# Reordering the head of a gated attention/MLP kernel: warm-up products, the first three transposes and the release of the DMA transposes

## The chip, the cores and the metric

The kernel runs on one core of a Trainium2 chip. The time is the device time of one execution in microseconds (us); the median of several runs is compared. A profiled execution has its own time and, a little shorter, a span from its first to its last instruction; all starts below are us from the beginning of that span. Engines are called PE (TensorE products), DVE (VectorE), ACT (ScalarE), POOL (GpSimd) and SP (SyncE, which here only issues DMAs).

## The reference, cut to what matters

x has 2048 rows (tokens) of 640 bf16 numbers. Two branches are computed from it and mixed by a gate:

```python
def _A_ref(x, wqkv, wo):          # linear attention, 32 heads of 20
    q, k, v = split(x @ wqkv)
    phi = lambda t: jnp.where(t > 0, t + 1, jnp.exp(t)) + 1e-6
    pq, pk = phi(q), phi(k)
    kv = einsum("bhsd,bhse->bhde", pk, v);  z = sum over s of pk
    o = (pq @ kv) / (pq . z + 1e-6)
    return o @ wo

def _B_ref(x, w1, w2, w3, w4):    # mixer with shifted tokens, then an MLP
    h = gelu(layernorm(x) @ w1);  hs = shift tokens of four column groups by 1, -1, 2, -2
    x1 = x + hs @ w2
    return x1 + gelu(layernorm(x1) @ w3) @ w4

g = sigmoid((x * gate_w).sum(-1))
return g * _A_ref(x, ...) + (1 - g) * _B_ref(x, ...)
```

The part that concerns us is the very first stage, the keys: x @ wk, with phi put on it. The gate's sum and a row sum of x are got from the same product, as two extra columns of the weight: `gate_w` and ones.

## The kernel before, in words

The 2048 tokens are 16 chunks of 128. A product on PE contracts over the partition axis, so the key product of a chunk needs x transposed: `xT[:, dc, chunk]`, five blocks of 128 of the 640 features (dc = 0 to 4). The same chunk is also loaded untransposed, as `x_sb`, for later use.

**Two ways to a transposed chunk.** Chunks 0, 1 and 2 are loaded plainly (`load_x`, L155) and turned on PE: `x_tr(c, a, b)` (L322) does five 128x128 transposes, three into PSUM tile `PP[a]` and two into `PP[b]`; DVE copies the three to `xT` and ACT the two (L327, L328). "Turn" below means this. Chunks 3 to 15 are turned by the DMA on the way in: `load_xT` (L158), a DMA transpose issued by SP. They are issued in `late_loads()` (L285) in the order of use, plain loads of `x_sb` between them: chunks 3, 4, x 3, chunks 5, 6, x 4-5, chunk 7, chunks 8-9, x 6-8, chunk 10, chunks 11-12, x 9-11, chunks 13-15, x 12-15, and then the weights wq, w1, wv, wo and w2. POOL's four copies of w1 to `w1x` (L312) stand at its end.

**What holds the DMA transposes.** DVE writes one zero into `xT` at the first element of chunk 3 (L333). The first DMA transpose writes the same place and so waits for that write; the rest stand behind it on SP's queue. DVE works in program order, so the zero is written when DVE has done what stands before it.

**PSUM.** There are four tiles `PP[0]` to `PP[3]`, each 128 x 1024 fp32. `free` lists those not in use; `alloc` takes the first of them, `release` appends one.

**The key product.** `k_mm(c, p, dc)` (L258) is two products, 512 and 130 columns wide (640 features, the gate column and the ones column), accumulated over dc in `PP[p]`. `k_post` (L263) does phi (ACT, then DVE twice) and releases the tile. The gate column of the weight comes from `g5`, a load of gate_w as 5 rows of 128, by one small transpose on PE (L318) and five one-column copies on DVE (L320).

**The order before.** PE first runs six products of zeros (`warm`, L316) while nothing has landed, then the gate's small transpose, the turn of chunk 0, the turn of chunk 1 (which shares `PP[2]` with the first), the key products of chunks 0 and 1 for dc = 0 and 1, the turn of chunk 2, the rest of the key products of chunks 0 to 2, and then chunks 3 to 15 in a loop (L351), with some products of the Gram matrix x^T pk (`g_unit`, L269) between from chunk 5 on. The zero write and `late_loads()` stand after the turn of chunk 0. The program order is kept as written on every engine; the framework adds the semaphore waits. After the keys come the queries (L393, which need wq), the two branches, and the MLP; none of that is touched.

Of the kernel before, what the change touches and what calls it, by code (L numbers as in the profile page):

```python
# [10 lines left out]
BF16 = mybir.dt.bfloat16  # L11
# [5 lines left out]
def kernel(  # L17
# [13 lines left out]
    nc = tc.nc  # L31
    P = 128
    S, D = A_x.shape[1], A_x.shape[2]
# [3 lines left out]
    DC = D // P  # L37
# [18 lines left out]
    def sb(name, cols, dt=BF16):  # L56
        return const.tile([P, cols], dt, name=name)
# [12 lines left out]
    def x1(c):  # L70
        return x1lo[:, c, :] if c < NCH // 2 else x1hi[:, c - NCH // 2, :]
# [5 lines left out]
    wkg = RA[:, 0:DC * KP].rearrange("p (j d) -> p j d", j=DC)  # L77
# [25 lines left out]
    w4z = shs[:, 512:640]  # L103
    w1x = sb("w1x", DC * P)[:].rearrange("p (j d) -> p j d", j=DC)
    kvT = sb("kvT", 6 * GW)[:].rearrange("p (g d) -> p g d", g=6)
    warm = sb("warm", 512)
    ident = sb("ident", P)
    onec = sb("onec", 1)
    mask32 = sb("mask32", 32)
# [2 lines left out]
    g5 = sb("g5", P)  # L112
# [23 lines left out]
    PP = [psum.tile([P, 1024], F32, name=f"pp{i}") for i in range(4)]  # L136
    free = [0, 1, 2, 3]

    def alloc():
        return free.pop(0)  # L140

    def release(i):
        free.append(i)

    mm = nc.tensor.matmul
# [57 lines left out]
    def stats(mv, c, src):  # L203
        st = bst[c % 2]
        h = D // 2

        def a():
            nc.vector.bn_stats(st[:, 0:6], src[:, 0:h])

        def b():  # L210
            nc.vector.bn_stats(st[:, 6:12], src[:, h:D])
            nc.vector.bn_aggr(mv[:, c, :], st[:].rearrange("p (k s) -> p k s", s=6))
        return a, b
# [35 lines left out]
    def phi(dst, src, n, extra=None):  # L249
        e = eb[ecnt[0] % NE]  # L250
        ecnt[0] += 1
        act(e[:, 0:n], src, ACT.Exp)  # L252
        if extra is not None:
            act(extra[0], extra[1], ACT.Copy)
        nc.vector.tensor_scalar(e[:, 0:n], e[:, 0:n], 1.0, 1e-6, op0=ALU.min, op1=ALU.add)  # L255
        nc.vector.scalar_tensor_tensor(dst, src, 0.0, e[:, 0:n], op0=ALU.max, op1=ALU.add)  # L256

    def k_mm(c, p, dc):  # L258
        for (n0, n1) in ((0, 512), (512, KW)):
            mm(PP[p][:, n0:n1], lhsT=xT[:, dc, c * P:(c + 1) * P], rhs=wkg[:, dc, n0:n1],  # L260
               start=(dc == 0), stop=(dc == DC - 1))

    def k_post(c, p):  # L263
        phi(pk[:, c, :], PP[p][:, 0:D], D, (ym[:, c, :], PP[p][:, D:D + 2]))
        release(p)
# [19 lines left out]
    def late_loads():  # L285
        load_xT(3, 4)
        load_xT(4, 5)
        load_x(3, 4)
        load_xT(5, 6)
        load_xT(6, 7)  # L290
        load_x(4, 6)
        load_xT(7, 8)
        load_xT(8, 10)
        load_x(6, 9)
        load_xT(10, 11)
        load_xT(11, 13)
        load_x(9, 12)
        load_xT(13, 16)
        load_x(12, 16)
        rows = lambda w, a, b: w[:, a:b].rearrange("(j p) d -> p j d", p=P)  # L300
        sp.dma_start(wq, rows(A_wqkv, 0, D))
        sp.dma_start(w1, rows(B_w1, 0, D))
        sp.dma_start(wv, rows(A_wqkv, 2 * D, 3 * D))
        sp.dma_start(wo6[0:GW, 0:5, :], A_wo[0:5 * GW, :].rearrange("(g r) d -> r g d", r=GW))
        sp.dma_start(wo6[0:GW, 5, :], A_wo[G5:D, :])
        sp.dma_start(w2[:, 0:4, :], B_w2.rearrange("(g c) d -> c g d", c=CG)[0:P])
        for g in range(4):
            sp.dma_start(w2[32 * g:32 * (g + 1), 4, :], B_w2[CG * g + P:CG * (g + 1), :])
        w1g = w1.rearrange("p k (g c) -> p k g c", c=CG)
        w1x4 = w1x.rearrange("p k (g c) -> p k g c", g=4)  # L310
        for g in range(4):
            nc.gpsimd.tensor_copy(w1x4[:, :, g, :], w1g[:, :, g, P:CG])  # L312


    for _ in range(6):
        mm(PP[3][:, 512:1024], lhsT=warm[:, 0:P], rhs=warm[:], start=True, stop=True)  # L316
    tg = PP[0][:, 512:1024].bitcast(BF16)
    nc.tensor.transpose(tg[:, 0:DC], g5[0:DC, :], ident[0:DC, 0:DC])  # L318
    for dc in range(DC):
        nc.vector.tensor_copy(wkg[:, dc, D:D + 1], tg[:, dc:dc + 1])  # L320

    def x_tr(c, a, b):  # L322
        ta, tb = PP[a][:, 0:512].bitcast(BF16), PP[b][:, 0:512].bitcast(BF16)
        for dc in range(DC):
            t, k = (ta, dc) if dc < 3 else (tb, dc - 3)
            nc.tensor.transpose(t[:, k * P:(k + 1) * P], x_sb[:, c, dc * P:(dc + 1) * P], ident[:])  # L326
        nc.vector.tensor_copy(xT[:, 0:3, c * P:(c + 1) * P], ta[:, 0:3 * P].rearrange("p (j s) -> p j s", j=3))  # L327
        act(xT[:, 3:5, c * P:(c + 1) * P], tb[:, 0:2 * P].rearrange("p (j s) -> p j s", j=2), ACT.Copy)  # L328

    for _ in range(3):  # L330
        alloc()
    x_tr(0, 3, 2)
    nc.vector.memset(xT[:, 0, 3 * P:3 * P + 1], 0.0)  # L333
    late_loads()
    x_tr(1, 1, 2)
    k_mm(0, 0, 0)
    k_mm(1, 1, 0)
    k_mm(0, 0, 1)
    k_mm(1, 1, 1)
    x_tr(2, 3, 2)  # L340
    k_mm(2, 2, 0)
    k_mm(2, 2, 1)
    for c in range(3):
        k_mm(c, c, 2)
    for c in range(3):
        for dc in (3, 4):
            k_mm(c, c, dc)
        k_post(c, c)


    for c in range(3, NCH):  # L351
# [35 lines left out]
    for half in range(2):  # L387
        for j in range(DC):
            p = alloc()
            for dc in range(DC):  # L390
                for tt in range(2):
                    t0 = half * 1024 + tt * 512
                    mm(PP[p][:, tt * 512:(tt + 1) * 512], lhsT=wqp[:, dc, j], rhs=xT[:, dc, t0:t0 + 512],  # L393
                       start=(dc == 0), stop=(dc == DC - 1))
# [150 lines left out]
    for c in range(NCH):  # L545
        a, b = stats(mv2, c, x1(c))
# [174 lines left out]
```

## Time and profile before

| what | value |
|---|---|
| median of 4 runs | 265.44 us (264.67 to 265.91) |
| the profiled execution's own time | 265.32 us |
| its span | 263.6 us |
| PE busy | 257.0 us, 97% of the span |
| DVE, ACT, POOL busy | 48%, 42%, 14% |
| products of the key stage (L260) | 24.0 us of PE in 156 records |
| DMA transposes of x (L159) | 9 issues on SP, 1.2 to 3.4 us each |

The profile page lists the engines' busy time, the span in 40 slices, the chain of work that ended last and the costliest groups. The views used beside it are the list of waits of one engine, the timeline (instructions in order of time, alike neighbours merged: start, length, engine, line, operation, count, and in brackets the idle time before and what ended it), the answers for one tile (with the time from a DMA's issue to its landing), and the table of stretches (busy time of each engine, and in the last columns the granted clock, the busy share of the DMA engines and GB/s). "SPq" is SP's issuing of a DMA. A matmul's length in the timeline includes its way through the array; the distance from one start to the next is what it costs in a stream.

### The profile page before, as it was taken

To read this page: it belongs to the slowest core of one execution; us is meant where nothing else is said; L and a number is where in the kernel's file an instruction comes from. 1 tells how busy PE (TensorE), PEld (TensorE's weight loads), DVE (VectorE), ACT (ScalarE), POOL (GpSimd) and SP (SyncE) were. 2 spreads that over 40 slices of the span, in tenths; PEclk is the share of its full clock that TensorE was granted. 3 is DMA by queue.
4 is the path that set the end of the run, shared out by engine and by line. 5 is a ranking of instruction groups with operands and counts; after the bars stand their busy time and mean duration, and the time that the engine had idled before them with its cause. 6 is when DMAs were issued, how large, how long until landed. Compare 5 with 4: busy or idle time off the path is not lost.

```text
span 263.6 us, 4153 instructions
## 1 busy us (share of the span) xinstructions
PE 257.0 (97%) x1634; PEld 136.1 (52%) x1666; DVE 126.9 (48%) x227; ACT 109.7 (42%) x163; POOL 36.0 (14%) x120
## 2 busy tenths in 40 slices
PE   7999999999999999999999999999999999999995
PEld 3555555555564445554444455555544445555553
DVE  2387759888995257999920023422310002334133
ACT  3466654555353771334977432102034445202200
POOL 7000053030200000436770000000000000000000
DMA  6799995552252059992552000200200000010011
GB/s 203 146 217 225 371 244 135 100 52 47 53 59 43 4 139 373 340 187 50 100 103 50 0 2 0 75 27 0 77 25 0 0 2 0 0 51 26 25 52 50
DMA packets 42372, 24.07 MB, mean 91 GB/s; under 512 B 31137, under 2 KB 41585, under 8 KB 42353
## 3 DMA queue, kind: packets, MB, share of 16 engines
q1 hardware_dynamic: 41767, 23.28, 37.1%
q10 hardware_dynamic: 586, 0.53, 0.6%
q8 instruction: 13, 0.21, 0.4%
q14 instruction: 6, 0.05, 0.1%
HBM read 12.98 MB, written 3.44 MB: 62 GB/s over the span
## 4 chain that ended last, share of the span: by engine, by line
PE 97%; issue 1%; ACT 0%; DVE 0%
PE pp L632 21%; PE pp L576 20%; PE pp L260 8%; PE pp L606 8%; PE pp L269 8%; PE pp L426 8%; PE pp L561 8%; PE pp L393 8%; PE pp L585 2%; PE pp L316 1%; PE pp L638 1%; PE pp L595 1%; PE pp L446 1%; PE pp L458 1%; PE pp L326 1%
## 5 line engine op out<-in xcount | busy, mean ns | idle before, releaser
L632 PE MATMUL pp<-RB,RXH 128*128 128x128 bf16 (+1 forms) x407 | 57.7, 297 | 0.7 <-issue 0.3
L576 PE MATMUL pp<-lnxT,RA 128*128 128x512 bf16 x236 | 51.9, 379 | 0.2
L632 PEld LDWEIGHTS <-RXH 128*128 128x128 bf16 x416 | 31.8, 98 | 24.5
L576 PEld LDWEIGHTS <-RA 128*128 128x128 bf16 x240 | 23.4, 98 | 28.1
L578 ACT ACTIVATE RXH<-pp 128x1024 bf16<-128x1024 f32 x24 | 24.3, 1021 | 30.5 <-PE pp L576 30.5
L252 ACT ACTIVATE eb<-pp 128x640 bf16<-128x640 f32 (+1 forms) x26 | 21.4, 829 | 25.0 <-PE pp L393 16.1
L609 ACT ACTIVATE RXH<-pp,g_all 128x640 f32<-128x640 f32 x16 | 12.7, 795 | 45.4 <-PE pp L606 45.4
L611 DVE SCALAR_TENSOR_TENSOR RPK<-RPK,omg,RXH 128x640 f32<-128x640 f32 x8 | 7.1, 885 | 41.4 <-ACT RXH L609 41.4
L269 PE MATMUL pp<-RPK,RXH 128*128 128x512 bf16 (+1 forms) x158 | 25.1, 298 | 0.1
L260 PE MATMUL pp<-RA,RXT 128*128 128x130 bf16 (+1 forms) x156 | 24.0, 301 | 0.7 <-ACT RXT L328 0.5
L393 PE MATMUL pp<-RXT,RA 128*128 128x512 bf16 x98 | 23.1, 379 | 0.1
L606 PE MATMUL pp<-Mp,pqT 128*128 128x128 bf16 (+1 forms) x158 | 22.9, 298 | 0.1
L611 DVE SCALAR_TENSOR_TENSOR RXT<-RXT,omg,RXH 128x640 f32<-128x640 f32 x8 | 7.1, 884 | 32.0 <-ACT RXH L609 32.0
L561 PE MATMUL pp<-w,RXH 128*128 128x128 bf16 (+1 forms) x157 | 21.7, 297 | 0.2
L426 PE MATMUL pp<-lnxT,RB 128*128 128x512 bf16 x76 | 18.1, 379 | 0.2
L269 PEld LDWEIGHTS <-RXH 128*128 128x128 bf16 x160 | 12.7, 98 | 10.4
L260 PEld LDWEIGHTS <-RXT 128*128 128x128 bf16 x160 | 12.6, 99 | 10.2 <-DVE RXT L327 0.8
L606 PEld LDWEIGHTS <-pqT 128*128 128x128 bf16 x160 | 12.3, 98 | 9.8 <-issue 0.4
L561 PEld LDWEIGHTS <-RXH 128*128 128x128 bf16 x160 | 12.3, 98 | 9.6
L393 PEld LDWEIGHTS <-RA 128*128 128x128 bf16 x100 | 11.1, 117 | 9.1
L255 DVE TENSOR_SCALAR eb<-eb 128x640 bf16<-128x640 bf16 (+1 forms) x26 | 9.6, 367 | 11.4 <-ACT eb L252 11.4
L256 DVE SCALAR_TENSOR_TENSOR RPK<-pp,eb 128x640 bf16<-128x640 f32 x16 | 13.2, 824 | 2.1
(112 smaller groups left out, 237.9 us busy)
## 6 DMA issues: line engine op xcount, KB each, us to landing
out_dram<-RXH SPq DMA_DIRECT2D x15, 160.0 KB, 1.8
RA<-in_B_w_dram SPq DMA_DIRECT2D x5, 432.0 KB, 6.6
RA<-in_A_wqkv_dram SPq DMA_DIRECT2D x2, 800.0 KB, 6.7
RB<-in_B_w_dram SPq DMA_DIRECT2D x1, 1120.0 KB, 8.8
RXH<-in_A_x_dram SPq DMA_DIRECT2D x2, 480.0 KB, 4.8
RB<-in_B_w_dram SPq DMA_DIRECT2D x1, 960.0 KB, 11.0
RB<-in_B_w_dram SPq DMA_DIRECT2D x1, 800.0 KB, 8.4
Mp<-Mscr SPq DMA_DIRECT2D x1, 800.0 KB, 4.3
```

Of the source, the lines that this page charges most:

```text
L252: act(e[:, 0:n], src, ACT.Exp)
L256: nc.vector.scalar_tensor_tensor(dst, src, 0.0, e[:, 0:n], op0=ALU.max, op1=ALU.add)
L260: mm(PP[p][:, n0:n1], lhsT=xT[:, dc, c * P:(c + 1) * P], rhs=wkg[:, dc, n0:n1], start=(dc == 0), stop=(dc == DC - 1))
L269: mm(PP[p][:, n0:n1], lhsT=x_sb[:, c, i * P:(i + 1) * P], rhs=pk[:, c, n0:n1], start=(c == 0), stop=(c == NCH - 1))
L393: mm(PP[p][:, tt * 512:(tt + 1) * 512], lhsT=wqp[:, dc, j], rhs=xT[:, dc, t0:t0 + 512], start=(dc == 0), stop=(dc == DC - 1))
L426: mm(PP[p][:, tt * 512:(tt + 1) * 512], lhsT=lh, rhs=lnxT[:, dc, t0:t0 + 512], start=(dc == 0), stop=(dc == DC - 1))
L561: mm(PP[p][:, n0:n1], lhsT=hsT[:, fc, 2 + c * P:2 + (c + 1) * P], rhs=w2[:, fc, n0:n1], start=(fc == 0), stop=(fc == DC - 1))
L576: mm(PP[p][:, k * 512:(k + 1) * 512], lhsT=w3[:, dc, (fc + k) * P:(fc + k + 1) * P], rhs=lnxT[:, dc, t * 512:(t + 1) * 512], start=(dc == ...
L578: act(h2T[:, t % 2, fc:fc + 2, :], PP[p][:].rearrange("p (k s) -> p k s", k=2), ACT.Gelu_apprx_tanh)
L606: mm(PP[p][:, n0:n1], lhsT=pqT[:, j, c * P:(c + 1) * P], rhs=Mp[:, j, n0:n1], start=(j == 0), stop=(j == DC - 1))
L611: nc.vector.scalar_tensor_tensor(x1(c), x1(c), omg[:, c:c + 1], ga, op0=ALU.mult, op1=ALU.add)
L632: mm(PP[ps[m]][:, n0:n1], lhsT=h2T[:, k, fc, i * P:(i + 1) * P], rhs=w4[:, fc, n0:n1], start=(m < 2 and fc == 0), stop=(m >= 2 and fc == N ...
```

## The change

- The buffer of zeros `warm` has 16 columns instead of 512; the warm-up products read one column of it, broadcast to 128 and to 512.
- Five warm-up products stand before the turn of chunk 0, and one after it (before: six, all before it). They write `PP[1]`.
- `x_tr` is split: `x_tr` has the five PE transposes alone, `x_cp` the copies by DVE and ACT.
- The turn of chunk 0 uses `PP[3]` and `PP[2]` as before; the turn of chunk 1 uses `PP[1]` and `PP[0]` (before: 1 and 2); that of chunk 2 uses `PP[1]` and `PP[0]` again (before: 3 and 2).
- The gate's small transpose stands after the turn of chunk 0 and goes to the upper half of `PP[3]`; its five copies on DVE stand after DVE's copy of chunk 0.
- The turn of chunk 2 stands after the dc = 0 products of chunks 0 and 1; their dc = 1 products stand after it.
- The key products of chunks 0, 1, 2 accumulate in `PP[3]`, `PP[2]`, `PP[1]` (before: 0, 1, 2); chunk 3 finds `PP[0]` free.
- The zero write and `late_loads()` stand after the copies of chunk 2 (before: after those of chunk 0).

The number of instructions on PE is the same, 3334; everything from chunk 3 on is the same on every engine but for the names of the PSUM tiles.

```diff
--- before.py
+++ after.py
@@ -103,7 +103,7 @@
     w4z = shs[:, 512:640]
     w1x = sb("w1x", DC * P)[:].rearrange("p (j d) -> p j d", j=DC)
     kvT = sb("kvT", 6 * GW)[:].rearrange("p (g d) -> p g d", g=6)
-    warm = sb("warm", 512)
+    warm = sb("warm", 16)
     ident = sb("ident", P)
     onec = sb("onec", 1)
     mask32 = sb("mask32", 32)
@@ -312,40 +312,51 @@
             nc.gpsimd.tensor_copy(w1x4[:, :, g, :], w1g[:, :, g, P:CG])
 
 
-    for _ in range(6):
-        mm(PP[3][:, 512:1024], lhsT=warm[:, 0:P], rhs=warm[:], start=True, stop=True)
-    tg = PP[0][:, 512:1024].bitcast(BF16)
-    nc.tensor.transpose(tg[:, 0:DC], g5[0:DC, :], ident[0:DC, 0:DC])
-    for dc in range(DC):
-        nc.vector.tensor_copy(wkg[:, dc, D:D + 1], tg[:, dc:dc + 1])
+    def warm_up(n):
+        for _ in range(n):
+            mm(PP[1][:, 512:1024], lhsT=warm[:, 0:1].to_broadcast([P, P]), rhs=warm[:, 0:1].to_broadcast([P, 512]),
+               start=True, stop=True)
+
+    warm_up(5)
 
     def x_tr(c, a, b):
         ta, tb = PP[a][:, 0:512].bitcast(BF16), PP[b][:, 0:512].bitcast(BF16)
         for dc in range(DC):
             t, k = (ta, dc) if dc < 3 else (tb, dc - 3)
             nc.tensor.transpose(t[:, k * P:(k + 1) * P], x_sb[:, c, dc * P:(dc + 1) * P], ident[:])
+
+    def x_cp(c, a, b):
+        ta, tb = PP[a][:, 0:512].bitcast(BF16), PP[b][:, 0:512].bitcast(BF16)
         nc.vector.tensor_copy(xT[:, 0:3, c * P:(c + 1) * P], ta[:, 0:3 * P].rearrange("p (j s) -> p j s", j=3))
         act(xT[:, 3:5, c * P:(c + 1) * P], tb[:, 0:2 * P].rearrange("p (j s) -> p j s", j=2), ACT.Copy)
 
-    for _ in range(3):
-        alloc()
     x_tr(0, 3, 2)
+    tg = PP[3][:, 512:1024].bitcast(BF16)
+    nc.tensor.transpose(tg[:, 0:DC], g5[0:DC, :], ident[0:DC, 0:DC])
+    warm_up(1)
+    x_cp(0, 3, 2)
+    for dc in range(DC):
+        nc.vector.tensor_copy(wkg[:, dc, D:D + 1], tg[:, dc:dc + 1])
+    x_tr(1, 1, 0)
+    x_cp(1, 1, 0)
+    hp = (3, 2, 1)
+    del free[1:]
+    k_mm(0, 3, 0)
+    k_mm(1, 2, 0)
+    x_tr(2, 1, 0)
+    x_cp(2, 1, 0)
     nc.vector.memset(xT[:, 0, 3 * P:3 * P + 1], 0.0)
     late_loads()
-    x_tr(1, 1, 2)
-    k_mm(0, 0, 0)
-    k_mm(1, 1, 0)
-    k_mm(0, 0, 1)
-    k_mm(1, 1, 1)
-    x_tr(2, 3, 2)
-    k_mm(2, 2, 0)
-    k_mm(2, 2, 1)
+    k_mm(0, 3, 1)
+    k_mm(1, 2, 1)
+    k_mm(2, 1, 0)
+    k_mm(2, 1, 1)
     for c in range(3):
-        k_mm(c, c, 2)
+        k_mm(c, hp[c], 2)
     for c in range(3):
         for dc in (3, 4):
-            k_mm(c, c, dc)
-        k_post(c, c)
+            k_mm(c, hp[c], dc)
+        k_post(c, hp[c])
 
 
     for c in range(3, NCH):
```

## The prediction

> **What bounds the kernel now.** I read the page's busy times first, then PE's list of waits.
>
> ```profile
> PE 257.0 (97%) x1634; PEld 136.1 (52%) x1666; DVE 126.9 (48%) x227; ACT 109.7 (42%) x163; POOL 36.0 (14%) x120
> ```
>
> ```profile
> PE pp L316 <- DVE warm L161: 1.2, 1, 1.2
> PE pp L260 <- ACT RXT L328: 0.5, 1, 0.5
> ...
> PE pp L326 <- ACT RXT L328: 0.2, 1, 0.2
> ```
>
> PE is the bound, without a hole after the head. So whatever the head gains or loses reaches the end in full, and the forecast is the shift of PE's work behind the head. Its own idle time is small: 1.2 us before the first product, 0.2 in the turn of chunk 1, 0.5 behind the turn of chunk 2. Next the timeline of PE and of SP.
>
> ```profile
> 1.24 2.74 PE L316 MATMUL pp<-warm 128*128 128x512 bf16 x6 [1.24 <-DVE warm L161]
> ...
> 4.98 2.61 SPq L159 DMA_TRANSPOSE RXT<-in_A_x_dram  x2
> ...
> 7.63 0.58 SPq L156 DMA_DIRECT2D RXH<-in_A_x_dram  x1
> ...
> 7.85 7.25 PE L260 MATMUL pp<-RA,RXT 128*128 128x512 bf16 x51 [0.47 <-ACT RXT L328]
> 8.25 2.52 SPq L159 DMA_TRANSPOSE RXT<-in_A_x_dram  x2
> ...
> 10.82 0.58 SPq L156 DMA_DIRECT2D RXH<-in_A_x_dram  x1
> ...
> 11.45 2.67 SPq L159 DMA_TRANSPOSE RXT<-in_A_x_dram  x2
> ...
> 14.16 0.62 SPq L156 DMA_DIRECT2D RXH<-in_A_x_dram  x1
> ...
> 14.82 4.33 SPq L159 DMA_TRANSPOSE RXT<-in_A_x_dram  x2
> ```
>
> Add start and length of each SP row: from 4.98 us on the next begins within 0.05 us of the last one's end, and so on to 23.8. SP is a full queue; what starts it later makes all of it later. How near PE runs behind it is seen from the starts of chunks 8 and 10 and of the queries:
>
> ```profile
> 19.15 1.53 PE L260 MATMUL pp<-RA,RXT 128*128 128x512 bf16 x10
> 22.42 1.53 PE L260 MATMUL pp<-RA,RXT 128*128 128x512 bf16 x10
> 32.22 2.32 PE L393 MATMUL pp<-RXT,RA 128*128 128x512 bf16 x10
> ```
>
> and from the tile answer for the issue of chunks 8 and 9 alone, and the stretch 20 to 21 us:
>
> ```profile
> L159 SPq DMA_TRANSPOSE RXT<-in_A_x_dram x1: 1413/1413/1413, 12.7 to 12.7; - x1
> ...
> DMA to landing us min/median/max: 5.2/5.2/5.2
> ```
>
> ```profile
> 20.00:21.00 1.00, 1.00 (x9) 0.53 (x8) 0.87 (x2) 0.29 (x1) 0.00 (x0) 1.00 0.14 13
> ```
>
> Chunks 8 and 9 land at 12.71 + 5.15 = 17.86 and are used at 19.15: margin 1.29. The same sum for chunk 5 (issued 8.25, 3.8 to land): 12.07 against 13.57 (14.93, where the first Gram products start, less one chunk of 1.36): 1.50. For wq (issued 23.85, 6.7): 30.5 against 32.2: 1.7. For chunk 10 no view gives a landing; the trace's completion events put its last at 21.60, against 22.42: 0.82, the smallest, since the DMA engines moved almost nothing from 20 to 21 us (13 GB/s, share 0.14).
>
> **The change part by part.** I follow the new order with the durations of before.
>
> *Smaller zeros.* DVE's write of `warm` took 0.27 us; the nearest small one (L333) took 0.06. PE starts at 1.03 instead of 1.24. Broadcast operands have no row; the nearest is the warm-up product itself, six in 2.74 us with the last one 0.63 long, so 0.427 each. Bounds 0.21 (the rate of the same shape later) and 0.6; I take 0.427.
>
> *One warm-up product fewer ahead.* 1.03 + 5 x 0.427 = 3.17, and x's first chunk had its last completion at 3.12. With the 0.14 us that PE lost before at the same change of operand (3.78 to 3.91), the turn of chunk 0 starts at 3.30 instead of 4.03. Five transposes at 0.107: 3.81. Gate row 0.11, sixth product 0.43: 4.35, plus 0.14: 4.49. Chunk 1 landed at 4.33, so its turn runs from 4.49 to 5.0, and needs no PSUM tile back (before it waited 0.2). DVE copies chunk 0 from 3.84 to 4.20, then the gate column (five copies, 0.42 in sum) until 4.62, before PE wants it at 5.0 (cover 0.4; beyond that it would cost PE one for one). ACT's copy starts when its table load ends at 4.03 and is done at 4.4.
>
> *Products of chunks 0 and 1, dc = 0:* at the slow clock 0.427 + 0.107 each: 5.0 to 6.07. The weight's first block landed at 4.51; DVE's copy of chunk 1 ends at 5.39, before its product at 5.53. *Turn of chunk 2:* from 6.07 to about 6.5, with chunk 2 landed at 5.34. Its first three transposes have gone through at about 6.60 (third start 6.28 and 0.3). Then 13 pairs at 0.273 are left: 3.54. The two dc = 1 products lie over the copies of chunk 2 (0.545 us against 0.36 on DVE after 6.60), so the hole of 0.5 us is gone. PE stands before chunk 3 at 10.05. Before it was 14.93 - 3 x 1.363 = 10.84. This is the gain: 0.79 us, if its data is there.
>
> *The clock.* The view's granted clock says 1.00 all along, but products get nearer only at 6.3 us: pairs of 0.534 become 0.273. I take 6.3 for the changed kernel too. The Trainium skill ("TensorE: Matmul & The Clock Gate", PE-mode transpose) speaks against this: transposes don't count as PE activity for the clock, and the change puts turns between the warm-up products. If so the fast clock could come a window later (3.4 us by the same page's Part 1, no run here shows it): from 6.6 to 9.7 us 5.8 of the 13 pairs would go at 0.534, the other 7.2 at 0.273, and PE would reach chunk 3 at 11.7, 0.8 later than before. But see next: the transfers would hide nearly all of that; the sum would be 266.6 against 266.3.
>
> *The transposes held.* The zero write moves behind DVE's copy of chunk 2. Before, that copy's counterpart began at 4.57 and SP's first transpose at 4.98, 0.41 later. Now 6.60 + 0.41 = 7.01: SP starts 2.0 us later, and with it the nine DMA transposes, five loads of x between them, and wq, w1, wv, wo, w2. Only SP stands behind this write; DVE's next work is phi of chunk 0. POOL's copies of w1 waited until 32.8 and end 2 us later, ahead of the layernorm's small operations; the first result of these that DVE needs is used at 41.1 and was held by an ACT operation at 40.2, so 2.9 us cover it. wv, wo and w2 are used after 80 us.
>
> Can the queue catch up? The row first: SP spent 1.30 and 1.26 us on the first two issues and 1.21 on later single ones, so at best 0.1 comes back. The Trainium skill ("DMA: Bandwidth & Descriptors", Latency and other measured facts) gives a DMA transpose 261 GB/s, an estimate of 0.63 us for a chunk of 164 KB and 8.2 for thirteen; with the plain loads at the 368 GB/s of the stretch from 28 to 34 us, 5.8 more. That is 14 us where this trace took 20 (first issue 4.98, last transpose landed 25.5), so by the page the 2 us would be made up by about chunk 8, and the sum would be 264.5 to 265.8. In the trace the issues set the pace, so I hold to the row.
>
> So with a shift of 1.9 to 2.0, and 0.05 from landing to start: chunk 4 waits 0.2; chunk 5 starts 12.07 + 1.95 + 0.05 = 14.07, 0.5 later than before; chunk 8 at 19.86, 0.7 later; chunk 10 at 23.6, 1.2 later; the queries would be free at +0.3 and stay at +1.2. These are not added; the largest stays. 0.79 gained turns into about 1.0 lost: chunk 10's 1.2 if the pause falls as before, chunk 8's 0.7 if not, taken nearer the first. **Sum:** 265.32 + 1.0 = 266.3, which is 0.9 above the median of 265.44 (0.3%).
>
> **Rivals.** *The transfers stay hidden (faster).* Chunk 10's margin decides: as PE comes 0.8 earlier, a shift over zero eats the gain and one over 0.8 loses. For 264.5 the queue must have made up its 2 us by chunk 10, by shorter issues at less load, as the page's rate allows. Against it: SP's unbroken rows. *Chunk 10's pause doesn't come back.* The engines' idle stretch belongs to the moment and not to the order: chunks 5 and 8 bind, +0.5 to +0.7: 265.9. For it: nothing in the program asks for the pause. *The pause hits chunks 8 and 9.* Such a pause (1.5 us, as the gap in chunk 10's landings from 20.0 to 21.5) moves their landing from 19.8 to 21.3, against 19.15: +2.1, or 267.4, taken as 267.3. *The clock comes a window late:* 266.6.
>
> **How the numbers follow.** Forecast 0.50, hidden transfers 0.06, no pause 0.26, pause on chunks 8 and 9 0.10, late clock 0.08. The measurement can tell about 0.3% (0.8 us) from no change. Faster by that: only hidden transfers, 0.06. Slower: pause on 8 and 9, late clock, and 0.38 of the forecast's 0.50, as its 0.9 stands just above 0.8: 0.55 with rounding down. Within: 0.39. The likeliest case alone spans 265.8 to 266.8; the range takes in no pause and the pause on 8 and 9 and leaves out most of the hidden case: 265.2 to 267.3.
>
> **What would show it.** The first SP transpose at about 7.0 instead of 4.98; the turn of chunk 0 at 3.3; no wait for ACT on PE around 7 us; PE waits for DMA landings on `RXT` at chunks 4, 5, 8 and 10, of about 0.2, 0.9, 0.2 and 0.5 us; the queries at 33 to 33.5 instead of 32.22. Wrong it would be if the transposes land less than 1 us later than before at chunks 8 to 10, or if the warm-up products of broadcast operands run at another rate.

## The result

The changed kernel takes 266.61 us (median of 44 runs, 265.32 to 268.12), the kernel before 265.33 (63 runs). The ratio is 1.0043, with a 95% interval from 1.0032 to 1.0055: slower by 1.14 us (0.0043 x 265.3). The profiled execution took 266.15 us with a span of 264.4, against 265.32 and 263.6.

PE's list of waits in the changed kernel:

```profile
PE pp L260 <- DVE RPK L256: 1.5, 1, 1.5
PE pp L317 <- DVE warm L161: 1.0, 1, 1.0
PE pp L260 <- DMA RXT<-in_A_x_dram: 0.4, 1, 0.4
PE pp L643 <- issue: 0.3, 2, 0.2
```

The two waits for ACT in the head are gone, as the change means them to be. Two waits in the key products (L260) have come, of 0.4 and 1.5 us. The page of the profile says that a wait for several semaphores may be put down to the wrong one; where the 1.5 us come from is seen in the timeline of PE:

```profile
0.98 2.31 PE L317 MATMUL pp<-warm 128*128 128x512 bf16 x5 [0.98 <-DVE warm L161]
3.19 0.71 PE L326 MATMUL pp<-ident,RXH 128*128 128x128 bf16 x5
...
5.91 3.71 PE L260 MATMUL pp<-RA,RXT 128*128 128x512 bf16 x25
10.00 4.35 PE L260 MATMUL pp<-RA,RXT 128*128 128x512 bf16 x30 [0.39 <-DMA RXT<-in_A_x_dram]
...
16.09 0.71 PE L269 MATMUL pp<-RPK,RXH 128*128 128x512 bf16 x4
18.33 1.54 PE L260 MATMUL pp<-RA,RXT 128*128 128x512 bf16 x9 [1.53 <-DVE RPK L256]
...
33.05 2.32 PE L404 MATMUL pp<-RXT,RA 128*128 128x512 bf16 x10
```

The row at 10.00 is chunk 3: PE was ready for it at 9.45 (the last product of chunk 2 started at 9.40 and takes 0.056), 1.4 us ahead of the 10.84 before. The row at 18.33 is chunk 7. Its DMA transpose, in the tile's answer for that issue alone:

```profile
L159 SPq DMA_TRANSPOSE RXT<-in_A_x_dram x1: 1211/1211/1211, 12.9 to 12.9; - x1
...
DMA to landing us min/median/max: 5.4/5.4/5.4
```

12.88 + 5.41 = 18.29, and PE starts at 18.33: it waited for this landing, not for DVE. In the kernel before the same transpose was issued at 11.45 and took 4.0 us. Its answer for that issue, and PE's row for chunk 7:

```profile
DMA to landing us min/median/max: 4.0/4.0/4.0
...
17.52 1.53 PE L260 MATMUL pp<-RA,RXT 128*128 128x512 bf16 x9
```

So PE comes to chunk 7 0.8 us later than before (17.52), the queries start at 33.05 instead of 32.22, and the span is 0.8 us longer. The difference made at 18 us is the difference at the end.

SP's part of the timeline:

```profile
6.41 2.61 SPq L159 DMA_TRANSPOSE RXT<-in_A_x_dram  x2
...
12.88 2.57 SPq L159 DMA_TRANSPOSE RXT<-in_A_x_dram  x2
...
16.13 4.14 SPq L159 DMA_TRANSPOSE RXT<-in_A_x_dram  x2
...
24.70 0.51 SPq L301 DMA_DIRECT2D RA<-in_A_wqkv_dram  x1
```

The queue starts at 6.41 instead of 4.98 (1.43 later), is 1.43 late at chunk 7 (12.88 against 11.45) and 0.85 late at wq (24.70 against 23.85).

Chunk 7's landing is 2.84 us later than before, twice the lateness of its issue. What lies between is a pause of the transfers. The table of stretches, from 16.5 to 17.5 us (last column: GB/s), and the DMA queues from 16.1 to 16.2 us:

```profile
16.50:17.50 1.00, 0.30 (x3) 0.00 (x0) 0.39 (x3) 1.00 (x3) 0.00 (x0) 1.00 0.97 33
```

```profile
q8 instruction: 1, 0.02, 75.5%
```

Almost nothing moves for a microsecond (33 GB/s), while the DMA engines count as busy (0.97). Just before, at 16.15 us, a single 16 KB packet starts on the queue that brings instructions, and takes 1.2 us; 18 packets of the transposes that start from 16.3 on take up to 1.7 us, where the usual one takes 0.02. In the kernel before the first such fetch came at 19.32 us and its long packets (16, up to 1.5 us) from 19.8 on.

### The profile page after: what moved, and what is told of

Its sections match the earlier page's. It is cut to its first block, busy times and chain, and to the rows that moved or that the text cites. A ratio compares the mean times of both kernels' runs of the same rounds, so it can differ in the third digit from the quotient of the medians.

```text
span 264.4 us, 4155 instructions
## 1 busy us (share of the span) xinstructions
PE 256.7 (97%) x1634; PEld 135.6 (51%) x1666; DVE 126.7 (48%) x227; ACT 109.8 (42%) x163; POOL 36.0 (14%) x120
## 4 chain that ended last, share of the span: by engine, by line
PE 96%; DMA 1%; issue 1%; DVE 1%; ACT 0%; DVEq 0%
PE pp L643 21%; PE pp L587 20%; PE pp L617 8%; PE pp L437 8%; PE pp L572 8%; PE pp L404 8%; PE pp L269 8%; PE pp L260 7%; PE pp L596 2%; DMA RXT<-in_A_x_dram 1%; PE pp L317 1%; PE pp L649 1%; PE pp L606 1%; PE pp L457 1%; PE pp L469 1%
## 5 line engine op out<-in xcount | busy, mean ns | idle before, releaser
L252 ACT ACTIVATE eb<-pp 128x640 bf16<-128x640 f32 (+1 forms) x26 | 21.4, 829 | 27.1 <-PE pp L404 16.1
L260 PE MATMUL pp<-RA,RXT 128*128 128x130 bf16 (+1 forms) x156 | 24.0, 299 | 2.1 <-DVE RPK L256 1.5
L260 PEld LDWEIGHTS <-RXT 128*128 128x128 bf16 x160 | 12.3, 98 | 11.9 <-DMA RXT<-in_A_x_dram 2.1
L437 PE MATMUL pp<-lnxT,RB 128*128 128x512 bf16 x76 | 18.1, 379 | 0.2
```

The costliest lines, as they stand in the source:

```text
L437: mm(PP[p][:, tt * 512:(tt + 1) * 512], lhsT=lh, rhs=lnxT[:, dc, t0:t0 + 512], start=(dc == 0), stop=(dc == DC - 1))
```

## The experiments

Two theories stand against each other. T: the late start of the DMA transposes costs, the rest of the new head gains. H: the new order of the head itself costs. A third question came from the profile: what makes the pause (theory F: the fetch of PE's instructions). Each ratio is to the kernel before, measured beside it.

### The changed kernel, released after chunk 0

```diff
     x_cp(0, 3, 2)
+    nc.vector.memset(xT[:, 0, 3 * P:3 * P + 1], 0.0)
+    late_loads()
     for dc in range(DC):
...
     x_cp(2, 1, 0)
-    nc.vector.memset(xT[:, 0, 3 * P:3 * P + 1], 0.0)
-    late_loads()
```

> The changed kernel with one part undone: the zero write and the late loads stand after the copies of chunk 0 again, all else stays. Theory T (the late start of the DMA transposes costs, the rest of the new order gains up to 0.8 us): SP's first transpose at about 4.5 us instead of 6.41 in the changed kernel and 4.98 in the one before; PE waits for no landing except perhaps 0.2 us, the queries start at 31.4 to 31.8 (32.22 before, 33.05 changed), and the time is 0.5 to 0.8 us under the kernel before, ratio 0.997 to 0.998. Rival H (the new order of the head itself costs, by its PSUM tiles or its warm-up products): the time stays above the kernel before, ratio 1.002 to 1.005, with the queries at 32.5 or later.

Measured: 264.38 us against 264.87, ratio 0.9981 (0.9968 to 0.9993). SP's first transpose came at 4.44, the queries at 31.41, and PE waited for no landing:

```profile
PE pp L317 <- DVE warm L161: 1.0, 1, 1.0
PE pp L643 <- issue: 0.3, 2, 0.2
```

Moving two lines back turns 1.14 us lost into 0.5 gained. H is out.

### The changed kernel, released after chunk 1

The same two lines behind `x_cp(1, 1, 0)`.

> The changed kernel with the zero write and the late loads after the copies of chunk 1, between the two other places. Theory T: SP's first transpose at about 5.3 us, 0.3 to 0.5 later than before; PE comes 0.8 earlier, so the margins of 0.8 to 1.5 us that the kernel before had are used up about exactly: waits of 0 to 0.5 us, ratio 0.997 to 1.000. Rival H: as the changed kernel, 1.002 to 1.005.

Measured: 264.15 us against 264.87, ratio 0.9974 (0.9957 to 0.9992). The first transpose came at 5.31, the queries at 31.18, and PE waited only 0.2 us, for a block of the weight. Its median is the lowest of all, but its interval overlaps that of the release after chunk 0. A start 0.3 us later than before costs nothing.

### The changed kernel, no hold

```diff
     nc.vector.memset(warm[:], 0.0)
+    nc.vector.memset(xT[:, 0, 3 * P:3 * P + 1], 0.0)
...
+    late_loads()
     warm_up(5)
```

> The changed kernel with no hold: the zero is written at the very start and the late loads stand right behind the first loads on SP. SP's first transpose at about 2.7 us. Theory T sees two effects: margins of the later chunks grow by 2 us, but the transposes' packets now lie among those of x chunk 2 and of the weight blocks, which landed at 5.3 to 7.1 us; with 0.6 to 1.3 us of transposes in front of them, these land at 6 to 8.5 and PE waits 0.5 to 1.5 us in the head. Ratio 0.997 to 1.002. A rival, contention rules (the hold is there because the early transposes would starve the weights): PE waits over 2 us in the head, ratio 1.004 or more.

Measured: 264.62 against 264.87, ratio 0.9987 (0.9968 to 1.0007). The first transpose was issued at 2.73, yet the weight's last two blocks landed at 6.84 and 6.88, no later than with the hold (6.75 and 6.91), and PE waited for none of them. The 0.5 to 1.5 us of waits that I expected of theory T in the head did not come: the transposes' first landing was at 7.33, behind the loads that had been issued before. So the hold protects nothing that this trace shows.

### The kernel before, released after chunk 2

The hold alone, on the old head: the two lines behind `x_tr(2, 3, 2)`.

> The kernel before with one part of the change alone: the zero write and the late loads after the turn and copies of chunk 2. Theory T: the copy of chunk 2 begins at 7.3, so SP's first transpose comes at 7.7, 2.7 us later than before; PE is where it was, so the smallest margin (0.8 to 1.3 us) is overrun by 1.4 to 1.9 us: ratio 1.005 to 1.007, PE waits for landings at chunks 5 to 10 of 1.4 to 1.9 us in sum. Rival H, or the transfers are hidden: ratio 0.999 to 1.001 and no wait.

Measured: 267.35 against 264.87, ratio 1.0086 (1.0055 to 1.0118), somewhat more than expected. SP's first transpose came at 7.26; PE's waits:

```profile
PE pp L260 <- DVE RPK L256: 1.5, 1, 1.5
PE pp L316 <- DVE warm L161: 1.2, 1, 1.2
PE pp L260 <- ACT RXT L328: 0.5, 1, 0.5
PE pp L260 <- DMA RXT<-in_A_x_dram: 0.5, 1, 0.5
```

Again one wait of 1.5 us, again at chunk 7, whose transpose (issued 13.73) took 5.5 us; the instruction fetch was at 16.57. The hold alone costs 2.3 us; in the changed kernel the new head pays about half of it back, in part because it reaches the release sooner (SP starts at 6.41 instead of 7.26).

### The kernel before, released after chunk 1

> The kernel before with the zero write and the late loads after the turn and copies of chunk 1 instead of chunk 0: a small dose of the hold on the old head. Theory T: SP's first transpose at about 5.5 us, 0.5 later than before; the smallest margin that the trace of before showed was 0.8 us, so nothing waits: ratio 0.999 to 1.001. If every delay of the transposes cost in proportion (a rival that sees no slack), 0.5 us: 1.002.

Measured: 265.24 against 265.12, ratio 1.0004 (0.9979 to 1.0030). The dose was smaller than meant: since the fast clock came early in the profiled execution, the first transpose stands at 5.13, only 0.15 us later than before. Nothing waited. It does not contradict the margin, but tests it weakly.

### The kernel before, turn of chunk 2 ahead of the dc = 1 products

```diff
     k_mm(1, 1, 0)
+    x_tr(2, 3, 2)
     k_mm(0, 0, 1)
     k_mm(1, 1, 1)
-    x_tr(2, 3, 2)
```

> The kernel before with the turn of chunk 2 ahead of the dc = 1 products of chunks 0 and 1, nothing else. The prediction's step: the 0.47 us in which PE waited for ACT behind the turn of chunk 2 is filled: 0.4 to 0.5 us gained, ratio 0.998 to 0.9985, and PE's wait for ACT gone from its list. If the margins of the transfers are already used up, PE waits for a landing instead and the ratio is 1.000.

Measured: 264.43 against 265.12, ratio 0.9976 (0.9961 to 0.9990): 0.6 us gained. PE's waits:

```profile
PE pp L316 <- DVE warm L161: 1.2, 1, 1.2
PE pp L632 <- issue: 0.3, 2, 0.2
PE pp L326 <- ACT RXT L328: 0.3, 1, 0.3
```

The 0.5 us behind the third turn are gone and no landing has taken their place, since SP's first transpose stays at 4.87. This one exchange is as good as the best version of the whole new head.

### The kernel before, small zeros and five warm-up products

```diff
-    warm = sb("warm", 512)
+    warm = sb("warm", 16)
...
-    for _ in range(6):
-        mm(PP[3][:, 512:1024], lhsT=warm[:, 0:P], rhs=warm[:], start=True, stop=True)
+    for _ in range(5):
+        mm(PP[3][:, 512:1024], lhsT=warm[:, 0:1].to_broadcast([P, P]), rhs=warm[:, 0:1].to_broadcast([P, 512]),
+           start=True, stop=True)
```

> The kernel before with the small buffer of zeros and five warm-up products of broadcast operands ahead of the gate row and the first turn, none behind. The prediction's step: the first turn starts at about 3.4 us instead of 4.03, the products of chunk 0 at about 5.0 instead of 5.38: 0.3 to 0.4 us gained, ratio 0.9985 to 0.999. If the clock rises later for want of the sixth product, up to 1 us lost: 1.000 to 1.003.

Measured: 265.09 against 265.12, ratio 1.0004 (0.9978 to 1.0029). The expected 0.3 to 0.4 us did not show, but the interval does not exclude it either. The first turn came at 3.34 as expected. In the profiled execution chunk 1 then landed 0.5 us later than in the trace of before (PE waited 0.8 us for it), and the products became fast only at 9.7. An earlier first turn is worth little, as the second one waits for its landing anyway.

### Released after chunk 1, without the product between the turns

The changed kernel with the two lines behind `x_cp(1, 1, 0)` and `warm_up(1)` taken out.

> The second kernel of the first job (release after chunk 1) without the one warm-up product between the turns of chunks 0 and 1. If that product only fills time until chunk 1 lands: same within 0.2 us, ratio 0.996 to 0.999. If it is what brings the fast clock in time: the clock rises a window later, 0.5 to 1.5 us lost, ratio 0.999 to 1.004.

Measured: 265.22 against 265.43, ratio 0.9984 (0.9968 to 1.0000). The interval lies across both expectations. In its profile chunk 2 and two weight blocks landed late (PE waited 0.7 us for chunk 2); no link of this to the missing product is seen. The first fast product came at 5.3 us, as it did with the product in place (5.4), so in this one profile the fast clock did not need it. What that product is worth in time stays open.

### The changed kernel, warm-up products cut into four

Each product of 512 columns becomes four of 128; the key stage is untouched.

```diff
-    warm_up(5)
+    warm_up(20)
...
-    warm_up(1)
+    warm_up(4)
```

> The changed kernel with each warm-up product of 512 columns cut into four of 128: the same time on PE, but 36 instructions more ahead of the key stage (18 products and 18 weight loads). It tests what the pause of the transposes comes from. Theory F (a 16 KB fetch of PE's instructions, one for each 256 of them, holds the transposes' packets for 1 to 2 us while it lasts): the first such fetch moves by 36 instructions, from 16.15 us in the changed kernel to 13.0 to 14.0, the long packets with it, and PE's long wait falls on chunk 5 or 6 instead of 7; the time stays within 0.4 us of the changed kernel's, ratio 1.002 to 1.006. Rival (the pause belongs to the order of the transfers): long packets and wait stay at chunk 7, 16.3 to 18.3 us.

Measured: 266.79 against 265.12, ratio 1.0060 (1.0041 to 1.0080). The first 16 KB fetch moved from 16.15 to 12.14 us (further than expected), and 21 packets of the transposes that started at 12.9 took up to 1.7 us. PE's timeline from 11 to 19 us:

```profile
10.73 1.53 PE L260 MATMUL pp<-RA,RXT 128*128 128x512 bf16 x10
14.65 2.86 PE L260 MATMUL pp<-RA,RXT 128*128 128x512 bf16 x10 [2.39 <-DMA RXT<-in_A_x_dram]
```

The long wait is at chunk 5 now, and there is none at chunk 7. The pause went with the fetch; the order of the transfers had not changed. The time of this kernel holds something else besides: after the long wait the products ran at half the clock (last section), and six of its 19 runs, at 267.6 to 268.3 us, show the mean clock of that profile, 0.994.

### The changed kernel, 60 small warm-up products

```diff
-            mm(PP[1][:, 512:1024], lhsT=warm[:, 0:1].to_broadcast([P, P]), rhs=warm[:, 0:1].to_broadcast([P, 512]),
+            mm(PP[1][0:64, 512:576], lhsT=warm[:, 0:1].to_broadcast([P, 64]), rhs=warm[:, 0:1].to_broadcast([P, 64]),
...
-    warm_up(5)
+    warm_up(48)
...
-    warm_up(1)
+    warm_up(12)
```

> The changed kernel, hold and all, with its six warm-up products of 512 columns replaced by 60 of 64 x 64 (48 ahead of the first turn, 12 behind it): 108 instructions more on PE ahead of the key stage, at about the same or 0.5 us more time. The hold is untouched. Theory F (the fetch of PE's instructions makes the pause): the first 16 KB fetch comes at 6 to 8 us, before or as the first transposes' packets start (about 8 us), so no burst of 1 to 2 us packets follows at 13 to 20 us from it, chunk 7 lands by 17.0, PE waits under 0.6 us in sum for landings, and the time comes down to within 0.4 us of the kernel before: ratio 0.998 to 1.002. Rival (the pause belongs to the order or the late start of the transfers): PE's wait of about 1.5 us stays at chunk 7, ratio 1.003 to 1.006.

Measured: 266.77 against 265.43, ratio 1.0057 (1.0035 to 1.0080): the expected time was missed. The fetch came at 7.79, within the stretch that I had named, but it was not early enough: 20 packets that started from 8.7 on took up to 1.3 us, and they were those of the first transpose, of chunk 3. PE's waits and its timeline from 9 us on:

```profile
PE pp L260 <- DMA RXT<-in_A_x_dram: 1.4, 1, 1.4
```

```profile
8.74 1.25 PE L260 MATMUL pp<-RA,RXT 128*128 128x512 bf16 x8
11.40 1.79 PE L260 MATMUL pp<-RA,RXT 128*128 128x512 bf16 x12 [1.41 <-DMA RXT<-in_A_x_dram]
```

The whole wait is at chunk 3; none is left at chunk 7. So three kernels with the same hold and the same order of transfers have their long wait at chunks 7, 5 and 3, each behind the fetch (16.15, 12.14, 7.79), and none is faster for it. Where the pause falls decides where PE waits. A version with the hold and no pause ahead of a tight chunk was not found, so what the hold would cost without the pause was not measured.

## Why the prediction was right

**The sum.** 1.0 us longer was forecast against the profiled execution; it was 0.83 (266.15 against 265.32), and 1.14 by the ratio. What carries the forecast came: nothing is lost in the head, all in waits for late landings, and the difference at one chunk, here chunk 7, is the difference at the end. That the size fits is in part luck. The hold was 0.6 us shorter than forecast, and by the prediction's own sum that leaves 0.66 late at chunk 10 (1.43 + 0.05 - 0.82) instead of 1.2; the rest came because the pause fell on another chunk, for another reason, than the prediction had it. An estimate from the two traces: with the 4.0 us of before, chunk 7 would have landed at 16.9 (12.88 + 4.0) and PE would have started it 0.6 us ahead of the kernel before; the pause turned this into 0.8 us behind.

**The gain of the head** was put at 0.79 us to chunk 3. It was 1.39 in the profile, because the clock rose at 5.3 us and not at 6.3, which was the trace of before's and is no property of either kernel (see below). The filled hole was rightly sized: 0.4 to 0.5 expected, 0.6 measured alone (interval 0.3 to 1.0). The start of PE (0.98 against 1.03 worked out) and of the first turn (3.19 against 3.30) were right; that they are worth 0.3 us was not shown.

**The transposes held.** 7.01 us was forecast for SP's first transpose, 6.41 measured, again by the early clock: DVE's copy of chunk 2 began at 6.00 instead of 6.60, and SP came 0.41 behind it, as worked out. That the hold is the cause is shown from both sides: taken away it gives 0.9981 and 0.9974, alone 1.0086.

**"At best 0.1 comes back"** was too strict: it was read from issues of 1.21 to 1.30 us, while that of chunk 10, also a single chunk, took 1.90 in the kernel before. The queue was 1.43 us late at its start and 0.85 at wq, so 0.6 came back, all of it after chunk 7: chunk 10 and chunks 11-12 were issued in 4.14 us instead of 4.33, chunks 13-15 in 3.09 instead of 3.36, chunks 8-9 in 0.1 less. The estimate from 261 GB/s (the Trainium skill, "DMA: Bandwidth & Descriptors", Latency and other measured facts, a rate measured on one kernel) would have had the queue in time by chunk 8 and the thirteen chunks through in 14 us; they took 20.0 from the first issue to the last landing (20.6 before), and up to chunk 7, where it was decided, nothing came back.

**Which chunk binds** was wrong. The prediction let the idle stretch fall on chunk 10 as before, or on chunks 8 and 9; it fell on chunk 7, which had 2.07 us to spare (15.45 to 17.52) and with a hold of 1.43 would not have waited by the prediction's way of reckoning. The failed step is that I read the pause as belonging to a transfer or to the moment, with "nothing in the program asks for the pause". Something does: the fetch of PE's own instructions. The forecast waits of 0.2, 0.9, 0.2 and 0.5 us at chunks 4, 5, 8 and 10 were 0.4 at chunk 3, 0.1 at chunk 5 and 1.5 at chunk 7; their sum, 1.8 forecast and 2.0 measured, was near.

**The rivals.** Hidden transfers: the landings were 2.8 us later where the margin was 2.1. Of the clock the rule that turns don't count as activity (the Trainium skill, "TensorE: Matmul & The Clock Gate", PE-mode transpose) made no difference to be seen: with turns between the products the clock rose at 5.3 in the profile, and the late rise did not come. This does not test the rule itself.

## What to carry to other kernels

Before a queue is held back, subtract the hold from the smallest margin behind it (landing to use), not from the first use: here chunk 3 could spare 3 us, chunk 8 1.3 and chunk 10 only 0.8. A margin read from one trace holds for the pauses of that trace: when the pause moved to chunk 7 here, that chunk took 5.4 us to land instead of 4.0. A hole on PE is best filled by moving independent products into it, which here took one exchange and left the DMA queue where it was. Take a wait's name in the list of waits as a hint and compare with the landing: the 1.5 us put down to DVE were a DMA's.

## What the runs showed of the hardware

**A fetch of PE's instructions holds up the DMA transposes in flight.** PE runs 3334 instructions here and the instruction queue shows 13 packets of 16 KB, one for each 256. In eleven of the twelve profiles transposes' packets that usually take 0.02 us became long, the longest 1.2 to 1.9 us, and the first of them started within 0.9 us of the first fetch, while its packet was still under way; in two of the eleven only three packets were long. In the changed kernel released after chunk 1 they came 1.9 us behind it (16.01 and 17.88), when the fetch was over (17.32), and need not be its own. Putting 36 and 108 instructions more on PE moved the fetch by 4.0 and 8.4 us and the pause by 3.4 and 7.6. SP's issuing is held as well: in the run with 36 more, a plain load issued at 12.18 took 1.94 us to issue, where 0.58 is usual. Not every pause has such a fetch: in the kernel before another one, of 1.1 us at 15.6, has none that the profile records, and three more profiles show one like it before 19 us; their cause is open.

**A wait of 2.4 us was followed by half the clock.** In the run with the wait of 2.39 us the products after it ran at half speed, by the table of stretches (the last three columns are the granted clock, the DMA share and GB/s):

```profile
13.00:14.00 1.00, 0.00 (x0) 0.00 (x0) 0.87 (x2) 0.78 (x3) 0.00 (x0) 1.00 0.89 17
14.00:15.00 1.00, 0.35 (x1) 0.13 (x2) 0.87 (x3) 0.00 (x0) 0.00 (x0) 0.84 0.37 66
14.65:17.30 2.65, 2.65 (x11) 1.27 (x12) 0.63 (x1) 0.00 (x0) 0.00 (x0) 0.50 0.93 211
```

Clock 0.50 for chunk 5, which took 2.65 us instead of 1.36. The half clock lasted from 14.7 to 18.1 us, 3.4 us, and lowers the mean clock of the 266 us to 0.994 (1 - 0.5 x 3.4 / 266). The waits of 1.4 and 1.5 us in the other profiles did not do this. Three of the 44 runs of the changed kernel have a mean clock of 0.994 too, at 267.5 to 268.1 us; by this estimate each had one such stretch. The 34 at a clock of 1.000 have a median of 266.57, so the result does not rest on them.

**The first rise of the clock moves by microseconds from run to run.** In the twelve profiles the first fast product of 512 columns in the key stage (0.38 us long instead of 0.63) began between 4.8 us and 9.7: on the old head between 5.1 and 9.7, on the new one between 4.8 and 6.9. In five of them the stage's first product is fast already, so the rise came earlier still. The granted clock in the table shows 1.00 for the slow ones too. One profile's head is therefore a sample; half a microsecond there is told by many runs, not by one trace.
